# Attention and two expert layers on one core: the first expert weights' loads and the first two narrowed weight units are placed later in the attention

## The chip, the cores and the metric

One core of a Trainium2 chip. The metric is the device time in microseconds (us) of one execution of the whole program. The median of three runs of the kernel before is 1269.96 us (1268.87 to 1276.14).

The engines are named TensorE (PE in the rows, PEld for its weight loads), VectorE (DVE), ScalarE (ACT), GpSimd (POOL) and SP, the sync engine, which here only issues DMAs. Each engine works through its own list of instructions in order; semaphores make it wait for others.

## The reference

The program computes three layers in a row, in float32:

```python
scores = q @ k.T / 8                         # 4 batches x 8 heads, 576 x 576, head size 64
kth = 32nd largest of each row               # keep the 32 largest scores of a row
attn = softmax(where(scores >= kth, scores, -1e9)) @ v
x = attn as 2304 rows x 512
# layer 2: top-1 of 8 experts (512 -> 1024 relu -> 512), for rows with x @ w_skip > 0
e = argmax(x @ w_gate); y = softmax(..)[e] * (relu(x @ w1[e]) @ w2[e]); x = x + y
# layer 3: 512 -> 1536 -> 512, gated
out = (silu(x @ moe2_gate) * (x @ moe2_val)) @ moe2_out
```

The three weight matrices of layer 3 reach the kernel as 64-bit floats. The kernel must turn them into 32-bit ones itself.

## The kernel before

**Attention.** Heads are taken in pairs. There are 16 pairs (4 batches x 4) and 9 tiles of 128 score rows in each, so 144 tiles. Batches 0 and 1 are group 0 (tiles 0 to 71), batches 2 and 3 are group 1. For each tile, `head` (lines 213 to 220) computes the scores on TensorE into PSUM, and ScalarE copies them out (`sc`, L219). Then `rows_tile` (lines 222 to 262) finds the 32 largest of each row: VectorE takes the larger of the two halves (L230), GpSimd computes the smaller (L244, L245), and VectorE goes four times through top-8 (L235, L248), with a match-replace in between that strikes out what was found (L247). For tiles 0 to 80 the mask is then made on ScalarE and TensorE (L255, L259, L260). `late` transposes the weights and multiplies by v. At most three tiles' scores are made ahead.

`prep` (lines 113 to 169) is a generator that loads k and q of a pair (`load`, L123 the first 512 rows of a head, L131 the rest), splits them in two parts on GpSimd (L157, L160, L161), transposes them, and at the end loads v (L123, L129). It is started nine tiles ahead: at tile 36 for the pair that begins at tile 45. It then goes one step a tile, so that v is loaded five tiles after k and q.

**The order.** The program is written as one stream, tile by tile, and each piece gets its priority by its place in the stream. A scheduler then makes the list of each engine before the run. It takes what is ready by its own model of the times, the oldest first; so an instruction that waits for nothing can come much earlier in its list than its place in the program. `issue_after(i)` binds the instructions of a block on the engine of `i` to come behind `i` in that engine's list. It does not make them wait for its end, and it binds no other engine.

**The driver.** `run` (lines 615 to 705) pulls the attention forward. Its first loop (lines 641 to 651) covers tiles 0 to 80. Once per tile, after the tile's work, it adds other work:

- *Narrowed units.* Layer 3's weights are cut into 18 units. `split_gated` and `gated_unit` (lines 563 to 594) make one unit: two loads of 512 KB of 64-bit words (L581), three VectorE instructions that turn them into 32-bit floats (`narrow`, L611 to L613), a rounded copy on ScalarE (L590), the remainder on GpSimd (L591), and two stores into a DRAM scratch `w2s` (L593 the whole, L592 the two parts). The first ND1 = 2 units are made in the first loop, in one buffer named `dec`, so that the second's loads wait for the first's stores. Before, unit 0 is asked for ahead of tile 0 (line 637) and unit 1 at tile 1 (line 645). The other units are made in the second part.
- *First weights.* `whole_weights` (lines 596 to 605) loads 1 MB of the first expert into one of four buffers of the ring `whl` (L604). Four such loads are asked for at tiles 40 to 43 (lines 648 and 649). Nothing else uses these buffers before, and nothing in the program binds the loads to a place.

From tile 81 on a second loop mixes the rest of the attention with group 0's experts (`moe1_whole`), the other units and group 0's layer 3 (`moe2`). After the attention come group 1's experts (`moe1`, whose weights are loaded as `wraw`) and group 1's layer 3.

Of the kernel before, what the change touches and what calls it, by code (L numbers as in the profile page):

```python
# [16 lines left out]
P = 128  # L17
NEG = -3.0e38
# [14 lines left out]
class Kernel:  # L33
# [79 lines left out]
    def prep(self, R, b, h):  # L113

        nc, sb, D, S = self.nc, self.at, self.D, self.S

        first = self.npair == 0

        def load(nm, t, i, parts=(0, 1)):
            src, eng = self.a[nm], nc.sync  # L120
            o = src.offset + (b * self.H + h + i) * S * D
            if 0 in parts:
                eng.dma_start(t[:, i, :4, :].rearrange("p c d -> p (c d)"),  # L123
                              bass.AP(tensor=src.tensor, offset=o, ap=[[4 * D, P], [1, 4 * D]]))
            if 1 not in parts:
                return
            tail = bass.AP(tensor=src.tensor, offset=o + 512 * D, ap=[[D, 64], [1, D]])
            if nm == "v":
                eng.dma_start(t[:64, i, 4, :], tail)  # L129
            else:  # L130
                eng.dma_start(t[i * 64:(i + 1) * 64, 0, 4, :], tail)  # L131

        kT = [sb.tile([P, S], F32R, name="kT", bufs=4) for _ in range(2)]
        qT = [sb.tile([P, 2, 512], F32R, name="qT", bufs=4) for _ in range(2)]
        qt = self.qt[self.npair % 2]
        self.npair += 1
        R.update(kT=kT, qT=qT, qt=qt)
        raws = {nm: sb.tile([P, 2, 5, D], F32, name="raw", bufs=2) for nm in ("k", "q")}
        for nm in ("k", "q"):
            load(nm, raws[nm], 0)  # L140
            load(nm, raws[nm], 1, (1,))
        for nm in ("k", "q"):
            load(nm, raws[nm], 1, (0,))
        nat = None
        for i in range(2):
            for nm, w in (("k", 2), ("q", 3)):
                if nat:
                    self.prep_t(*nat)
                n = 5 - i
                t = sb.tile([P, 5, 3 * D], F32R, name="nat", bufs=1)  # L150
                o = t[:, :n, :w * D].rearrange("p c (t e) -> p c t e", t=w)
                src = raws[nm][:, i, :n, :]
                if first:
                    for z in range(0, w, 2):
                        nc.scalar.activation(o[:, :, z, :], src, AF.Copy)
                elif w == 3:
                    nc.gpsimd.tensor_scalar(o[:, :, 0:3:2, :], src[:, :, None, :].to_broadcast([P, n, 2, D]),  # L157
                                            1.0, 1.0, op0=OP.mult, op1=OP.mult)
                else:
                    nc.gpsimd.tensor_scalar(o[:, :, 0, :], src, 1.0, 1.0, op0=OP.mult, op1=OP.mult)  # L160
                (nc.vector if first else nc.gpsimd).tensor_tensor(o[:, :, 1, :], src, o[:, :, 0, :].bitcast(F32),  # L161
                                                                  op=OP.subtract)
                nat = (nm, i, t, kT, qT, qt)
                yield
        self.prep_t(*nat)
        yield
        R["v"] = raw = sb.tile([P, 2, 5, D], F32, name="vv", bufs=3)
        for i in range(2):
            load("v", raw, i)
# [52 lines left out]
    def rows_tile(self, R, i, c, Z, on_pe, sc):  # L222
        nc, S = self.nc, self.S
        sb = self.at1 if on_pe else self.at
        W = S // 2
        scf = sc.rearrange("p a b -> p (a b)")
        rest = sb.tile([P, 2, W], F32, name="rest", bufs=3)
        hj, lo = rest[:, 0], rest[:, 1]
        hi = sb.tile([P, W], F32, name="hi", bufs=3)
        nc.vector.tensor_tensor(hi, sc[:, 0, :], sc[:, 1, :], op=OP.max)  # L230
        pair, n = divmod(self.nlx, 9)
        tops = self.tops[pair % 2]
        h, kth = tops[:, n, :], tops[:, n, 31:32]
        self.nlx += 1
        nc.vector.max(h[:, 0:8], hi)  # L235
        nb = sb.tile([P, 1], F32, name="nb", bufs=5)
        nc.gpsimd.tensor_scalar(nb, h[:, 0:1], -0.125 / BIG, 1.0, op0=OP.mult, op1=OP.mult)
        pp = sb.tile([P, S], F32, name="pp", bufs=3)
        if not on_pe:
            e = sb.tile([P, S], F32, name="e", bufs=2)  # L240
            nc.scalar.activation(e, scf, AF.Exp, bias=nb, scale=0.125 / BIG)
        sm = sb.tile([P, W], I32, name="sm", bufs=2)
        sci = sc.bitcast(I32)
        nc.gpsimd.tensor_tensor(sm, sci[:, 0, :], sci[:, 1, :], op=OP.add)  # L244
        nc.gpsimd.tensor_tensor(lo.bitcast(I32), sm, hi.bitcast(I32), op=OP.subtract)  # L245
        for j in range(1, 4):
            nc.vector.match_replace(hj, h[:, (j - 1) * 8:j * 8], hi if j == 1 else hj, NEG)  # L247
            nc.vector.max(h[:, j * 8:(j + 1) * 8], hj if j < 3 else rest.rearrange("p a b -> p (a b)"))  # L248
        if n == 8:
            nc.gpsimd.tensor_tensor(self.FL[:, self.nlx - 9:self.nlx], tops[:, :, 23], tops[:, :, 31], op=OP.subtract)  # L250
        if not on_pe:
            nc.vector.scalar_tensor_tensor(pp, scf, kth, e, op0=OP.is_ge, op1=OP.mult, accum_out=Z)  # L252
            return pp
        u = sb.tile([P, 2, W], F32R, name="e", bufs=3)
        nc.scalar.activation(u, sc, AF.Relu, bias=kth, scale=-1.0)  # L255
        pS = self.ps1.tile([P, 2, 512], F32, name="pM", bufs=1)
        self.scores(R, i, c, pS, stop=False)
        for x in range(2):
            nc.tensor.matmul(pS[:, x, :W], self.nidr, u[:, x, :], start=False, stop=True)  # L259
        nc.scalar.activation(pp.rearrange("p (a b) -> p a b", a=2), pS[:, :, :W], AF.Exp, bias=nb, scale=0.125,  # L260
                             accum_out=Z)
        return pp
# [352 lines left out]
    def run(self):  # L615
        nc = self.nc
        with ExitStack() as st:
# [5 lines left out]
            ring = Ring(self.pool(st, "ring"), 0, 4)  # L623
            with ExitStack() as s1:
                tmp = self.pool(s1, "tmp")
                self.at1 = self.pool(s1, "attn1")
                self.nidr = self.at1.tile([P, P], F32R, name="nidr")
                nc.vector.tensor_scalar(self.nidr, self.idn, -1.0, None, op0=OP.mult)
                self.ps1 = self.psum_pool(s1, "ps1")
                self.rps = (self.ps1, "pR", 1)  # L630
                w = None

                def early():
                    nonlocal w
                    self.late_constants(tmp)
                    w = self.split_gated(tmp, range(ND1), ("dec",))
                    next(w)

                self.early = early
                ready = []  # L640
                for t, f in att:
                    if f < 1:
                        continue
                    if t % 2:
                        next(w, None)
                    if t == half + 8:
                        break
                    if t >= 40 and len(ready) < 4:
                        ready.append(self.whole_weights(ring, 0, len(ready)))
                for _ in w:  # L650
                    pass
            mo = Moe(self, self.pool(st, "moe"), self.psum_pool(st, "pm"), 3, ring, 2)
# [6 lines left out]
            w = self.split_gated(mo.mo, mid, ("h2h", "h2l"))  # L659
# [554 lines left out]
```

## Time and profile before

| | |
|---|---|
| median of three runs | 1269.96 us (1268.87 to 1276.14) |
| the profiled execution, whole | 1265.73 us |
| its span, first to last instruction | 1264.0 us |
| mean granted TensorE clock | 0.980 |
| TensorE busy | 1195.6 us (95%) |
| VectorE busy | 994.6 us (79%) |
| ScalarE busy | 741.2 us (59%) |
| GpSimd busy | 684.8 us (54%) |
| mean DMA rate | 173 GB/s |

The shares are over the whole span and hide that stages have different limits. Tiles 0 to 80 take about the first 325 us. An idle time is put down to what ended it last. TensorE's ends are modelled, so that a TensorE that reads 100% may still have room.

### The profile page before, as it was taken

To read this page: it belongs to the slowest core of one execution; us is meant where nothing else is said; L and a number is where in the kernel's file an instruction comes from. 1 tells how busy PE (TensorE), PEld (TensorE's weight loads), DVE (VectorE), ACT (ScalarE), POOL (GpSimd) and SP (SyncE) were. 2 spreads that over 40 slices of the span, in tenths; PEclk is the share of its full clock that TensorE was granted. 3 is DMA by queue.
4 is the path that set the end of the run, shared out by engine and by line. 5 is a ranking of instruction groups with operands and counts; after the bars stand their busy time and mean duration, and the time that the engine had idled before them with its cause. 6 is when DMAs were issued, how large, how long until landed. Compare 5 with 4: busy or idle time off the path is not lost. (4 is left out here: it accounts for less than half of the span.)

```text
span 1264.0 us, 21890 instructions
## 1 busy us (share of the span) xinstructions
PE 1195.6 (95%) x7365; PEld 1026.5 (81%) x7366; DVE 994.6 (79%) x2327; ACT 741.2 (59%) x1622; POOL 684.8 (54%) x825
## 2 busy tenths in 40 slices
PE   5999999999899989999999999989999999999995
PEld 4778887788687868787877788779998789898994
DVE  6999999999998888989999974247887458184570
ACT  5899988999754545555544453137776435343430
POOL 6776766777654666556766553121221535555550
PEclk9999999999999999999998999989999999999998
DMA  6511111111277879865667755598988544543420
GB/s 205 181 39 39 39 39 39 34 36 38 78 257 278 288 267 300 283 206 188 225 235 243 274 189 164 187 329 263 305 277 277 175 156 132 166 134 118 147 78 28
DMA packets 126012, 219.10 MB, mean 173 GB/s; under 512 B 17860, under 2 KB 84420, under 8 KB 119620
## 3 DMA queue, kind: packets, MB, share of 16 engines
q1 hardware_dynamic: 118868, 178.84, 43.5%
q0 software_dynamic: 7024, 38.78, 9.3%
q8 instruction: 60, 0.98, 0.3%
q14 instruction: 60, 0.49, 0.1%
HBM read 177.75 MB, written 41.95 MB: 174 GB/s over the span
## 5 line engine op out<-in xcount | busy, mean ns | idle before, releaser
L248 DVE MAX8 tops<-rest 128x8 f32<-128x288 f32 (+1 forms) x432 | 231.2, 546 | 5.7 <-POOL rest L245 2.3
L1139 PE MATMUL m<-x2h,whl 128*128 128x384 f32 x576 | 197.3, 343 | 3.8 <-DVE th L1148 2.0
L1140 PE MATMUL m<-x2l,whl 128*128 128x384 f32 x576 | 195.8, 340 | 0.4 <-DVE x2l L1125 0.4
L1141 PE MATMUL m<-x2h,whl 128*128 128x384 f32 x576 | 196.0, 341 | 0.0
L1108 POOL TENSOR_TENSOR whl<-wfly,whl 128x1024 fp32r<-128x1024 f32 x54 | 129.8, 2404 | 107.4 <-ACT whl L1107 107.2
L244 POOL TENSOR_TENSOR sm<-sc 128x288 int32<-128x288 int32 x144 | 124.5, 865 | 61.9 <-ACT sc L219 58.8
L245 POOL TENSOR_TENSOR rest<-sm,hi 128x288 int32<-128x288 int32 x144 | 125.0, 868 | 53.5 <-DVE hi L230 43.7
L271 ACT ACTIVATE pt<-pT 128x512 f32<-128x512 f32 (+2 forms) x320 | 115.9, 404 | 37.0 <-PE pT L269 35.3
L1107 ACT ACTIVATE whl<-wfly 128x1024 fp32r<-128x1024 f32 x69 | 73.2, 1061 | 98.5 <-PE m L1141 59.0
L247 DVE MATCH_REPLACE8 rest<-tops,rest 128x288 f32<-128x288 f32 x288 | 125.9, 438 | 0.0
L280 PE MATMUL pT<-pt,vv 128*64 128x256 f32 (+3 forms) x640 | 121.1, 424 | 4.9 <-DVE L L441 2.9
L269 PE MATMUL pT<-idn,pp 128*128 128x128 f32 (+1 forms) x720 | 119.3, 281 | 1.0 <-ACT kT L186 0.5
L219 ACT ACTIVATE sc<-pS 128x576 f32<-128x576 f32 x144 | 93.4, 649 | 44.4 <-DVE pp L252 27.9
L1139 PEld LDWEIGHTS m<-x2h,whl 128*128 128x128 f32 x576 | 109.3, 190 | 7.0 <-DVE th L1148 2.6
L269 PEld LDWEIGHTS pT<-idn,pp 128*128 128x128 f32 (+1 forms) x720 | 79.7, 137 | 39.0 <-issue 26.9
L1141 PEld LDWEIGHTS m<-x2h,whl 128*128 128x128 f32 x576 | 109.6, 190 | 1.5 <-issue 1.3
L1140 PEld LDWEIGHTS m<-x2l,whl 128*128 128x128 f32 x576 | 109.3, 190 | 1.5 <-DVE x2l L1125 0.6
L209 PE MATMUL pS<-kT,qT 128*128 128x288 f32 x512 | 106.4, 326 | 1.7 <-ACT sc L219 0.9
L944 DVE TENSOR_TENSOR whl<-wraw,whl 128x1024 fp32r<-128x1024 f32 x64 | 78.4, 1239 | 34.8 <-ACT whl L943 34.2
L230 DVE TENSOR_TENSOR hi<-sc 128x288 f32<-128x288 f32 x144 | 96.5, 670 | 11.1 <-ACT sc L219 10.8
L1151 DVE TENSOR_TENSOR h2l<-th,h2h 128x384 fp32r<-128x384 f32 x36 | 85.9, 2386 | 21.5 <-ACT h2h L1150 21.5
L943 ACT ACTIVATE whl<-wraw 128x1024 fp32r<-128x1024 f32 x64 | 67.1, 1059 | 38.6 <-DMA wraw<-in_moe_w_dram 23.8
(213 smaller groups left out, 2885.4 us busy)
## 6 DMA issues: line engine op xcount, KB each, us to landing
wfly<-w2s SPq DMA_DIRECT2D x69, 512.0 KB, 3.7
whl<-in_moe_w_dram SPq DMA_DIRECT2D x32, 1024.0 KB, 7.5
wraw<-in_moe_w_dram SPq DMA_DIRECT2D x64, 512.0 KB, 5.1
whl<-w2s POOLq DMA_DIRECT2D x31, 1024.0 KB, 5.7
w2s<-h2h SPq DMA_DIRECT2D x8, 1024.0 KB, 6.1
w2s<-whl SPq DMA_DIRECT2D x8, 1024.0 KB, 8.5
io<-xa SPq DMA_DIRECT2D x18, 256.0 KB, 3.0
out_dram<-io SPq DMA_DIRECT2D x18, 256.0 KB, 3.6
```

The source lines that it names most:

```text
L209: m = self.nc.tensor.matmul(pS[:, x, :W], l, r[:, x * W:(x + 1) * W], start=(n == 0), stop=stop and n == len(ops) - 1)
L244: nc.gpsimd.tensor_tensor(sm, sci[:, 0, :], sci[:, 1, :], op=OP.add)
L245: nc.gpsimd.tensor_tensor(lo.bitcast(I32), sm, hi.bitcast(I32), op=OP.subtract)
L247: nc.vector.match_replace(hj, h[:, (j - 1) * 8:j * 8], hi if j == 1 else hj, NEG)
L248: nc.vector.max(h[:, j * 8:(j + 1) * 8], hj if j < 3 else rest.rearrange("p a b -> p (a b)"))
L269: self.anchor = nc.tensor.transpose(p[:k, c - a, :], pp[:, c * P:c * P + k], self.idn)
L271: nc.scalar.activation(T[:k, a:z, do:do + n], p[:k, :z - a, so:so + n], AF.Copy)
L280: self.anchor = nc.tensor.matmul(po[(n % 2) * D:(n % 2 + 1) * D, :W], v[:k, i, n, :], T[:k, n, :W], start=(n < 2), stop=(n >= 3))
L1108: self.fly_engine.tensor_tensor(lo, raw, hi.bitcast(F32), op=OP.subtract)
L1139: nc.tensor.matmul(pz, wh[:, z, k, :], xh[:, k, :], start=(k == 0), stop=False)
L1140: nc.tensor.matmul(pz, wh[:, z, k, :], xl[:, k, :], start=False, stop=False)
L1141: nc.tensor.matmul(pz, wl[:, z, k, :], xh[:, k, :], start=False, stop=(k == 3))
```

## The change

Unit 0 and unit 1 are no longer asked for ahead of tile 0 and at tile 1, but after tiles 22 and 31. The four loads keep their tiles, 40 to 43. Both now stand in a block with two bindings: what the block gives to SP comes, in SP's list, behind the last long load of a head traced so far (`self.loaded`), and what it gives to VectorE comes, in VectorE's list, behind the last match-replace traced so far (`self.mark`).

At tile 22 `self.loaded` is the last q load of the pair that begins at tile 27, at tile 31 that of the pair of tile 36, at tile 40 that of the pair of tile 45; at tiles 41 to 43 it is the second head's v load of the pair of tile 45.

```diff
@@ prep / load
             if 0 in parts:
-                eng.dma_start(t[:, i, :4, :].rearrange("p c d -> p (c d)"),
-                              bass.AP(tensor=src.tensor, offset=o, ap=[[4 * D, P], [1, 4 * D]]))
+                self.loaded = eng.dma_start(t[:, i, :4, :].rearrange("p c d -> p (c d)"),
+                                            bass.AP(tensor=src.tensor, offset=o, ap=[[4 * D, P], [1, 4 * D]]))
@@ rows_tile
         for j in range(1, 4):
-            nc.vector.match_replace(hj, h[:, (j - 1) * 8:j * 8], hi if j == 1 else hj, NEG)
+            self.mark = nc.vector.match_replace(hj, h[:, (j - 1) * 8:j * 8], hi if j == 1 else hj, NEG)
@@ run
                     w = self.split_gated(tmp, range(ND1), ("dec",))
-                    next(w)
...
                 for t, f in att:
                     if f < 1:
                         continue
-                    if t % 2:
-                        next(w, None)
+                    with self.tc.issue_after(self.loaded.ins), self.tc.issue_after(self.mark.ins):
+                        if t in (22, 31):
+                            next(w, None)
+                        if t >= 40 and len(ready) < 4:
+                            ready.append(self.whole_weights(ring, 0, len(ready)))
                     if t == half + 8:
                         break
-                    if t >= 40 and len(ready) < 4:
-                        ready.append(self.whole_weights(ring, 0, len(ready)))
```

## Rows read from the trace of the kernel before

**Rows 1.** The page's 40 slices of 31.6 us, tenths busy: VectorE.

```profile
DVE  6999999999998888989999974247887458184570
```

**Rows 2.** Waits of VectorE, 13 to 330 us: us in total, times, longest.

```profile
DVE hi L230 <- ACT sc L219: 5.2, 2, 5.1
```

**Rows 3.** Stretches: us, busy us (instructions) of the five, TensorE clock, DMA share, GB/s.

```profile
46.00:54.00 8.00, 8.00 (x58) 6.04 (x58) 8.00 (x16) 7.56 (x20) 6.66 (x8) 1.00 0.15 36
54.00:72.00 18.00, 15.99 (x113) 12.49 (x110) 18.00 (x59) 15.79 (x44) 15.38 (x25) 1.00 0.31 114
72.00:106.00 34.00, 34.00 (x255) 27.50 (x255) 34.00 (x108) 31.40 (x87) 24.63 (x42) 1.00 0.14 37
210.00:290.00 80.00, 79.35 (x595) 64.76 (x594) 80.00 (x254) 74.77 (x200) 58.23 (x98) 1.00 0.14 38
```

**Rows 4.** Stretch 210 to 290 us, L235 alone: us, VectorE busy (instructions), clock, DMA.

```profile
210.00:290.00 80.00, 9.79 (x22) 1.00 0.14 38
```

**Rows 5.** Tile dec, to 130 us: ns min/median/max, first and last start.

```profile
L611 DVE TENSOR_SCALAR dec<-dec x2: 681/940/1198, 18.8 to 46.1; 128x1024 int32<-128x1024 int32 x2
L612 DVE SCALAR_TENSOR_TENSOR dec<-dec x2: 1214/1271/1328, 21.1 to 48.4; 128x1024 int32<-128x1024 int32 x2
L613 DVE SCALAR_TENSOR_TENSOR dec<-dec x2: 1883/1888/1893, 24.4 to 51.5; 128x1024 int32<-128x1024 int32 x2
...
L590 ACT ACTIVATE dec<-dec x2: 1051/1054/1058, 26.3 to 53.4; 128x1024 fp32r<-128x1024 f32 x2
L591 POOL TENSOR_TENSOR dec<-dec x2: 2347/2364/2380, 28.2 to 55.4; 128x1024 fp32r<-128x1024 f32 x2
```

**Rows 6.** Lines L611, L612 and L613, whole span: the later units.

```profile
L611 DVE TENSOR_SCALAR h2h<-h2h x8: 669/694/1290, 339.6 to 517.5; 128x1024 int32<-128x1024 int32 x8
...
L612 DVE SCALAR_TENSOR_TENSOR h2h<-h2h x8: 1202/1216/1264, 342.1 to 519.3; 128x1024 int32<-128x1024 int32 x8
...
L612 DVE SCALAR_TENSOR_TENSOR whl<-whl,one x8: 1203/1267/1829, 578.7 to 702.6; 128x1024 int32<-128x1024 int32 x8
...
L613 DVE SCALAR_TENSOR_TENSOR h2h<-h2h x8: 1205/1210/1966, 345.0 to 521.5; 128x1024 int32<-128x1024 int32 x8
```

**Rows 7.** GpSimd by line, 72 to 140 us: busy us, mean ns, idle before.

```profile
L245 POOL TENSOR_TENSOR rest<-sm,hi 128x288 int32<-128x288 int32 x19 | 15.2, 803 | 7.5 <-DVE hi L230 7.5
```

**Rows 8.** SP's issues in order of time, 20 to 42 us: start us, us.

```profile
20.79 4.63 SPq L604 DMA_DIRECT2D whl<-in_moe_w_dram  x4
...
30.54 0.34 SPq L592 DMA_DIRECT2D w2s<-dec  x1
39.64 0.38 SPq L581 DMA_DIRECT2D dec<-in_moe_w_gate_dram  x1
```

**Rows 9.** Tile whl: landing of the first four loads (to 130 us); first reader.

```profile
DMA to landing us min/median/max: 10.7/11.8/13.0
...
L1072 PE MATMUL m<-whl,x2l x64: 379/379/634, 348.6 to 381.6; 128*128 128x256 f32 x64
```

**Rows 10.** Order of time: SP's issues 139 to 181 us, GpSimd's first use.

```profile
147.22 0.58 SPq L123 DMA_DIRECT2D raw<-in_q_dram  x1
...
167.24 0.58 SPq L123 DMA_DIRECT2D vv<-in_v_dram  x1
...
171.90 0.33 SPq L123 DMA_DIRECT2D raw<-in_k_dram  x1
...
184.75 0.46 POOL L160 TENSOR_SCALAR nat<-raw 128x320 fp32r<-128x320 f32 x1 [0.96 <-PE pR L185]
```

**Rows 11.** Stretch 30 to 40 us, columns as in rows 3.

```profile
30.00:40.00 10.00, 9.42 (x55) 7.96 (x56) 10.00 (x33) 8.69 (x19) 6.85 (x11) 0.75 0.84 303
```

**Rows 12.** TensorE in order of time, 24 to 33 us: [idle before <-releaser].

```profile
30.55 0.85 PE L259 MATMUL pM<-e,nidr 128*128 128x288 f32 x2 [3.78 <-ACT e L255]
```

**Rows 13.** Waits of SP's queue, to 180 us: us in total, times, longest.

```profile
SPq L410 <- DVE rz L408: 15.9, 1, 15.9
```

**Rows 14.** The chain that ended last: start us, us, what.

```profile
828.14 15.12 DMA wraw<-in_moe_w_dram
```

## The prediction

> **What bounds the kernel now.** The change touches only the first 81 of the 144 attention tiles, so the first question is which engine sets their pace. I read the page's slices first: VectorE is at nine tenths or more in every slice from the second to the thirteenth, which ends near 410 us [rows 1]. Then the waits of VectorE alone from 13 to 330 us: there is one entry, 5.2 us, and 5.1 of it is the first score tile's arrival [rows 2]. After that VectorE never waits for anybody for 300 us. The table by stretches says the same: 18.00 of 18.00, 34.00 of 34.00 and 80.00 of 80.00 us busy, while GpSimd and ScalarE have slack [rows 3]. TensorE shows 100% in two of these stretches too, but its ends are modelled, and it is short of that (15.99 of 18.00) where VectorE is not. So this stage is a queue of VectorE work. Its pace is the count of the first top-8 of each tile: 22 in 80 us, 3.64 us a tile [rows 4].
>
> **What the change moves, part 1: two narrowed units.** A unit costs VectorE three instructions (L611, L612, L613), ScalarE 1.05 us, GpSimd 2.36 us, and SP four DMAs: two loads, two stores. Before, both units lie between 18.8 and 58 us. Removed from there on VectorE: (0.681 + 1.198) + (1.214 + 1.328) + (1.883 + 1.893) = 8.2 us [rows 5]. All of it lies on the path, as the queue has no gap there: tiles 0 to 12 will be done up to 8.2 us earlier.
>
> The same six instructions come back behind the last match-replace of tiles 22 and 31, near 100 and 133 us. The queue is full there as well, so they are paid again. Their price is bounded by the later units of the same shape: at least 0.669 + 1.202 + 1.205 = 3.08 us a unit, at most 1.290 + 1.829 + 1.966 = 5.09 us [rows 6], for two units 6.2 to 10.2 us. The net of removal and return is therefore between -2.0 and +2.0 us. The long forms go with a busy GpSimd, and that is 85% busy (15.38 of 18.00) at 54 to 72 us, where the start still catches up, but 72% (24.63 of 34.00) where the units go [rows 3]. So I take -1 us.
>
> On L613 the two units took 1.89 us against 1.21 us at best, 0.68 us more, and a GpSimd instruction of a tile takes 0.80 us [rows 5 to 7]. The Trainium skill (SBUF — State Buffer, section "SBUF: two separate sides") has a rule for that: a VectorE instruction with two SBUF inputs and a GpSimd instruction that reads SBUF lock the same ports for a whole instruction, and the later one waits. The row agrees, being longer by less than one GpSimd instruction. By the rule alone, with none of L612 and L613 delayed before and all four delayed by a whole GpSimd instruction after, the sum would be 4 x 0.80 = 3.2 us the other way, an estimate with that page's lock.
>
> The rest of a unit is covered. ScalarE's 1.05 us and GpSimd's 2.36 us fall into stretches where these have 2.6 and 9.4 us free of 34 [rows 3]; uncovered, they would cost at most 2 x (1.05 + 2.36) = 6.8 us. The unit at 46 to 58 us is the nearest case of one placed into the running stage: VectorE had no gap there (8.00 of 8.00, then 18.00 of 18.00). TensorE was idle for 2 us afterwards and nobody lost by it [rows 3].
>
> SP issues its queue in order. Before, the second store of a unit was issued at 30.54 us, SP then stood until 39.64 us for the stores to land, as the one buffer has to be free, and only then came the next unit's loads [rows 8]. After the change the same standing falls behind tile 22. What is queued behind it is the next heads' q loads, then the tiny reciprocal load and the x stores. Loads of raw k at 171.90 us are read by GpSimd at 184.75 us [rows 10], so these loads run 10 us or more ahead, as much as SP stood. I cost it at nothing.
>
> **Part 2: the four 1 MB loads.** They were issued from 20.79 us, took 10.7 to 13.0 us to land, and nobody reads them before 348.6 us [rows 8, 9]. After the change the first can be issued right behind the q load at 147.22 us, the other three behind the v load at 167.24 us [rows 10]. Either place leaves some 170 us. Nothing at 20 to 33 us waits for a DMA that they delay, since VectorE has no gap, so their going gives nothing either. At the new place the raw k loads come behind three of them: three quarters of 13.0 us is 9.8 us, against the 12.8 us from issue to use. Hidden, with 3 us left; if that cover is gone, GpSimd stands and VectorE follows.
>
> **Part 3: clock and order.** Between 30 and 40 us the granted clock was 0.75 of full speed, half of that stretch at its lower level, 1.2 GHz instead of 2.4 [rows 11]. It fell after TensorE had waited 3.8 us, until 30.55 us, for a mask that VectorE made late, the narrowing being in between [rows 12]. The dip will be smaller or gone. That gives nothing, because VectorE did not wait for TensorE even then [rows 2]. From a profile of before no one can read how the list of instructions after tile 81 is re-sorted when the early part shifts; that is a rival below.
>
> **The sum.** The profiled execution took 1265.73 us (span 1264.0 and 1.7 around it). -8.2 + 7.2 (the units) + 0 (loads) + 0 (clock, SP) = -1.0, so 1264.7 us on its own scale. The median of the three runs shown is 4.2 us above that execution; on the scale of the median 1269 us. I forecast no change.
>
> **The rivals.** Times are on the median's scale; about 1% (12.7 us, so 1257.3 and 1282.7) is what a measurement of this kernel tells from no change.
>
> A, the start keeps its gain. If at tiles 22 and 31 TensorE and not VectorE set the pace, the 8.2 us would be hidden there: 1270 - 8.2 = 1262. For it: TensorE reads 34.00 of 34.00 at 72 to 106 us. Against it: a VectorE that is not the bound would wait, and it does not [rows 2]. 14%.
>
> B, VectorE stands in front of the second unit. The buffer is single, so unit 1 loads only after unit 0's stores have landed. In the trace of before from L613 of unit 0 (24.4 us, end 26.3) to L611 of unit 1 (46.1 us) went 19.8 us [rows 5]. From L611 to L611 lie nine tiles and one unit after the change, 9 x 3.64 + 4.1 = 36.9 us; less 7.3 us from L611 to the end of L613 (46.1 to 53.4 us for unit 1), 29.6 us are left, a margin of 9.8 us. SP's longest single wait is 15.9 us, for the reciprocals of a finished pair [rows 13], and one such wait falls between the two units. If SP puts the loads behind it, they are late by up to 15.9 - 9.8 = 6 us, and if the stores of unit 0 fall behind one too, by 6 + 9.8 = 16 us. VectorE's queue is in order, so it loses just that: 1276 to 1286. It decides from the point where L611 waits for a DMA at all. 12%, a third of it beyond 1%.
>
> C, the second half is sorted anew. The order of instructions on each engine is made before the run, by priorities and modelled times; a shift of some us at the start can put other instructions first where attention and experts are mixed. The size is that of the largest single wait on the chain that a changed order could remove or repeat: 15.12 us, TensorE for the first raw weights of the second group's experts [rows 14]. Either way: 1254 or 1285. Against it: after tile 31 both programs have the same work behind them, so the later order should be nearly the same. 18%: 9% down beyond 1%, 4% up beyond 1%, the rest small.
>
> D, the change doesn't do what it says: the edge behind the match-replace holds VectorE's instructions only, so scalar copies, splits and stores follow by their data, but the six narrowing instructions cannot run early. This would end in no change too. It is inside the forecast.
>
> **The numbers.** The forecast, 56%, holds 1268 to 1272 by the bounds of the units, and 1266 to 1274 with a little of their ScalarE and GpSimd work uncovered. With A (14%), B and C: faster by over 1% 0.10 (9% from C, 1% from A with some of C), slower 0.08 (4% from B, 4% from C), within 1% 0.82. The range reaches from A's 1262 down to half of C's way, 1259, and up to B's lower end with some of the rest, 1280; it leaves out about a tenth on each side.
>
> **What would show it.** Right: tile 12 done some 8 us earlier, tile 35 done within 2 us of before, L611 to L613 near 100 to 140 us at 3.1 to 5.1 us a unit, VectorE with no wait of over 1 us between 20 and 330 us, the four loads landing after 148 us. TensorE's full clock at 30 to 40 us without effect would confirm part 3. Wrong: tile 35 done 5 us or more earlier (A), a wait of VectorE for a DMA before L611 (B), GpSimd waiting for raw k near 185 us (part 2's cover gone), or equal times up to 330 us and a difference that arises later (C).

## The result and the profile after

The changed kernel takes 1256.48 us (median of 12 runs, 1250.97 to 1261.86), the kernel before, run beside it, 1268.21 us (12 runs, 1261.10 to 1276.14). The ratio is 0.991, with a 95% interval of 0.989 to 0.9931. I had forecast 1269.0 in a range from 1259 to 1280, so the time lies 2.5 us below the range. The profiled execution has a span of 1252.2 us (before 1264.0), a mean granted clock of 0.983 (0.980) and TensorE busy for 1193.1 us (1195.6).

The first stage came out as predicted. VectorE's slices of the page after, 31.3 us each:

```profile
DVE  6999999999999998989999973248888358183670
```

VectorE's waits after, from 13 to 330 us (us in total, times, longest) give the same single entry as before [rows 2]:

```profile
DVE hi L230 <- ACT sc L219: 5.2, 2, 5.1
```

The stretches after, columns as in [rows 3], where they have their counterparts (also [rows 11]):

```profile
30.00:40.00 10.00, 9.95 (x73) 8.42 (x71) 9.82 (x31) 8.90 (x23) 7.11 (x12) 0.93 0.05 16
46.00:54.00 8.00, 7.94 (x59) 6.20 (x57) 8.00 (x26) 7.63 (x22) 6.82 (x12) 1.00 0.01 2
...
72.00:106.00 34.00, 33.87 (x256) 27.71 (x256) 33.94 (x101) 31.80 (x89) 26.76 (x39) 1.00 0.27 82
106.00:143.00 37.00, 36.57 (x270) 29.58 (x268) 37.00 (x112) 33.90 (x88) 30.06 (x45) 1.00 0.30 95
210.00:290.00 80.00, 79.83 (x597) 65.48 (x596) 80.00 (x251) 74.23 (x200) 56.82 (x97) 1.00 0.13 35
```

VectorE is still without a gap, and the same 22 first top-8s of L235 fall into 210 to 290 us as in [rows 4]:

```profile
210.00:290.00 80.00, 9.74 (x22) 1.00 0.13 35
```

The two units now (tile dec after; ns min/median/max, first and last start us), against [rows 5]:

```profile
L611 DVE TENSOR_SCALAR dec<-dec x2: 679/880/1080, 98.3 to 133.6; 128x1024 int32<-128x1024 int32 x2
L612 DVE SCALAR_TENSOR_TENSOR dec<-dec x2: 1202/1202/1203, 100.4 to 136.0; 128x1024 int32<-128x1024 int32 x2
L613 DVE SCALAR_TENSOR_TENSOR dec<-dec x2: 1216/1440/1664, 102.7 to 138.3; 128x1024 int32<-128x1024 int32 x2
```

Their sum is (0.679 + 1.080) + (1.202 + 1.203) + (1.216 + 1.664) = 7.0 us, against 8.2 before. I call a tile done when its last top-8, the one of 576 elements (L248, 0.75 us), ends. Tile 12 is done at 64.2 us (before 71.2), tile 35 at 152.5 (152.9), tile 80 at 325.6 (326.6). So the 7 us of the start are paid back, and 1.0 us is left. This is one execution of each, and 1.0 us is within what kernels with nearly the same first stage differ by: tile 80 is done at 324.4 us in units_only and at 329.2 us in loads_only (experiment 1). VectorE, around tile 80, before and then after (start us, us):

```profile
325.87 0.75 DVE L248 MAX8 tops<-rest 128x8 f32<-128x576 f32 x1
```

```profile
324.86 0.74 DVE L248 MAX8 tops<-rest 128x8 f32<-128x576 f32 x1
```

SP after, in order of time: the stores of unit 1 (L593, L592) and the four 1 MB loads (L604) behind a q load.

```profile
142.11 0.58 SPq L123 DMA_DIRECT2D raw<-in_q_dram  x1
142.79 0.38 SPq L593 DMA_DIRECT2D w2s<-dec  x1
143.22 2.12 SPq L604 DMA_DIRECT2D whl<-in_moe_w_dram  x3
145.44 4.63 SPq L592 DMA_DIRECT2D w2s<-dec  x1
150.11 0.44 SPq L604 DMA_DIRECT2D whl<-in_moe_w_dram  x1
```

**Where the 12 us arise.** Behind tile 80 attention and the first group's experts share the engines, and TensorE is the busiest. One row of stretches from 330 to 520 us shows it (columns as in [rows 3]), before and then after:

```profile
330.00:520.00 190.00, 176.60 (x1028) 143.10 (x1026) 169.90 (x414) 97.19 (x227) 114.78 (x139) 0.96 0.80 268
```

```profile
330.00:520.00 190.00, 183.32 (x1088) 148.82 (x1088) 179.65 (x436) 105.86 (x247) 128.88 (x152) 0.98 0.85 283
```

In the same 190 us TensorE gets through 60 matrix instructions more. It idles 6.7 us instead of 13.4, and by the clock's records it runs 6.8 us at 1.2 GHz instead of 13.7, which is 3.4 us of work more. Together that is 10.1 us; with the 1.0 us of tile 80 it makes 11.1 of the 11.8 us by which the spans differ.

The traces also tell where the lead is complete. TensorE's last 4087 of its 7365 records are the same instructions in the same order before and after; they begin at 518.9 us before and at 505.8 us after, so the changed kernel is 13.1 us ahead there. The row of six L287 just behind that point, before and then after:

```profile
519.36 0.81 PE L287 MATMUL pT<-fold,oT 128*128 128x64 f32 x6
```

```profile
506.19 0.81 PE L287 MATMUL pT<-fold,oT 128*128 128x64 f32 x6
```

From there to the end the changed kernel takes 746.4 us and the kernel before 745.0, so about 1.3 us of the lead is lost again behind it. TensorE's waits from 345 to 510 us (us in total, times, longest), before:

```profile
PE m L1054 <- ACT th L1076: 4.7, 2, 3.4
PE m L1054 <- DMA io<-xa,ids: 4.5, 4, 2.5
```

and after:

```profile
PE m L1054 <- DMA io<-xa,ids: 1.8, 2, 1.3
PE pS L209 <- ACT sc L219: 1.8, 2, 1.5
PE m L1085 <- ACT x2h L1057: 1.0, 1, 1.0
```

The two largest waits of before, in order of time: the transposes of an expert's gathered rows (`io`), and those of its first layer's result (`th`), stand in TensorE's list before their input is there, and hold up what follows them.

```profile
389.93 1.03 PE L1054 MATMUL m<-idn,io 128*128 128x128 f32 x4 [2.53 <-DMA io<-xa,ids]
...
468.85 1.12 PE L1054 MATMUL m<-idn,th 128*128 128x128 f32 x4 [3.40 <-ACT th L1076]
```

### The profile page after: what moved, and what is told of

The parts are those of the page before. It is cut to its first block, busy times and chain, and to the rows that moved or that the text cites. A ratio compares the mean times of both kernels' runs of the same rounds, so it can differ in the third digit from the quotient of the medians.

```text
span 1252.2 us, 21888 instructions
## 1 busy us (share of the span) xinstructions
PE 1193.1 (95%) x7365; PEld 1024.1 (82%) x7366; DVE 990.3 (79%) x2327; ACT 742.4 (59%) x1622; POOL 690.6 (55%) x825
## 5 line engine op out<-in xcount | busy, mean ns | idle before, releaser
L248 DVE MAX8 tops<-rest 128x8 f32<-128x288 f32 (+1 forms) x432 | 230.8, 546 | 3.4
L1148 DVE SCALAR_TENSOR_TENSOR th<-th,m 128x384 f32<-128x384 f32 x72 | 39.1, 543 | 64.1 <-ACT th L1147 64.1
```

## The experiments

Ratios are to the kernel before, run beside each group (1267.6 to 1269.5 us), with 95% intervals. Diffs are against the changed kernel unless said otherwise. Kernels of different groups are best compared by these ratios, as the kernel before itself differs by up to 1.9 us between the groups. "Unit places" are the tiles behind which the two narrowed units are asked for (22 and 31 in the changed kernel).

**1. The units alone, and the loads alone.**

```diff
 units_only: the four loads as in before
-                        if t >= 40 and len(ready) < 4:
-                            ready.append(self.whole_weights(ring, 0, len(ready)))
...
+                    if t >= 40 and len(ready) < 4:
+                        ready.append(self.whole_weights(ring, 0, len(ready)))
 loads_only: the units as in before
+                    next(w)
...
+                    if t % 2:
+                        next(w, None)
-                        if t in (22, 31):
-                            next(w, None)
```

> Units at tiles 22 and 31 as in the changed kernel; the four 1 MB loads unbound as before. The lists of VectorE, TensorE, ScalarE and GpSimd are then those of the changed kernel, instruction for instruction; only SP's differs. Theory (the units' place re-sorts the lists, so that group 0's routing ends earlier and the experts start near 339 us instead of 349): within 3 us of the changed kernel, 1256, ratio to before 0.991. Rival (the gain is the 4 MB that no longer load at 20 to 33 us): 1266 to 1270, ratio 1.000.

> The two units at the start as before; only the four 1 MB loads bound behind the heads' loads. The routing stands at the same place in VectorE's list as before (the gates' product L541 after 85 tiles' first maxima). Theory: 1264 to 1271, ratio 1.000, first expert matmul within 3 us of 348.6 us. Rival (the loads' place is the gain): 1254 to 1260.

Measured: units_only 1255.87 us, 0.9894 [0.9867, 0.9921]; loads_only 1267.21 us, 0.9996 [0.9977, 1.0016]. The whole gain comes with the units' move, and the place of the four loads is worth nothing, as part 2 of the prediction had it. In units_only the lists of TensorE, VectorE, ScalarE and GpSimd are those of the changed kernel, instruction for instruction; only SP's differs.

**2. Later experts.** After the change the routing of group 0 and so the first expert's matrix instruction come earlier, at 338.9 us against 348.6 [rows 9]. Tile whl after, to 360 us:

```profile
L1072 PE MATMUL m<-whl,x2l x32: 378/379/483, 338.9 to 347.5; 128*128 128x256 f32 x32
```

My first theory was that this start carries the gain.

```diff
-            yield from self.first_slots(g, b, oh, sl, rows, gw)
+            yield from (*[0] * (3 * (g == 0 and b == 1)), *()); yield from self.first_slots(g, b, oh, sl, rows, gw)
...
-        nc.vector.tensor_tensor(v[:, :, :, 1], oh, gate...)                       # L541
+        with self.tc.issue_after(self.masked.ins) if (g, b) == (0, 1) else ExitStack(): (L541 as it was)
```

(`self.masked` is the last L252 traced.)

> The changed kernel with one instruction bound: the gates' product L541 of group 0's second batch comes in VectorE's list behind the masked weights L252 of the next tile, as it did in the kernel before. The lists are the same as in the changed kernel up to that instruction. Theory (the chain from this instruction over the first slots, the row numbers and the gather starts the experts): first expert matmul 5 to 8 us later than 338.9 us, the whole 4 to 8 us above the changed kernel, 1260 to 1264. Rival (the experts' start has slack, the gain is elsewhere): no change, 1256.

Measured: 1257.54 us, 0.9914 [0.9889, 0.9939]. The first expert instruction starts at 350.5 us, 11.6 us later than in the changed kernel, and the ratio is the same (0.991):

```profile
350.52 1.75 PE L1072 MATMUL m<-whl,x2l 128*128 128x256 f32 x7
```

This theory fell: an early start of the experts is not what carries the gain.

**3. Other places for the units.**

```diff
-                        if t in (22, 31):
+                        if t in (31, 40):   # units_31_40;  (40, 49), (49, 58), (61, 70), (13, 22) likewise
```

> The changed kernel with the units at tiles 31 and 40 instead of 22 and 31. By the lists the routing falls one tile later than in the changed kernel (L541 after 85 tiles' first maxima, as before). Theory (the routing's place in the list decides, whatever brings it there): first expert matmul near 346 to 350 us, 1263 to 1270. Rival (units anywhere behind the start give the gain, because the pause of VectorE lets TensorE catch up): 1254 to 1258.

> The changed kernel with the units at tiles 49 and 58. By the lists the row numbers of group 0 (L557) stand where they stand in the changed kernel, after 85 tiles' first maxima and 83 finished tiles, one tile ahead of before. Theory (the place of the routing in the list decides): TensorE's work at 400 us at least 6 us ahead of before, 1254 to 1261. Rival (TensorE's catching up behind tiles 22 and 31 is what counts, as 31 and 40 were slow): 1266 to 1274.

> The changed kernel with the units at tiles 61 and 70. By the lists L557 stands after 85 first maxima and 82 finished tiles, the earliest of all. Theory: first expert matmul at 342 us or earlier, TensorE's work at 400 us at least 8 us ahead of before, 1250 to 1260. Rival (a pause of VectorE so near to the end of the stage is not made up for, and the experts start later): 1264 to 1272.

> The changed kernel with the units at tiles 40 and 49. By the lists L557 stands after 86 first maxima and 84 finished tiles, as before and as with the units at 31 and 40. Theory: no gain, TensorE's work at 400 us within 6 us of before, 1263 to 1273. Rival (any place behind the start but the one tried gives the gain): 1253 to 1260.

> The changed kernel, with the two units behind tiles 13 and 22 instead of 22 and 31. In VectorE's list the routing step L541 stands behind the same tile as in the changed kernel. If that place goes with the gain (it does in the changed kernel, with the units alone moved, and with tiles 49 and 58): 1253 to 1260. If it is only the accident of where the lists interleave: between 1254 and 1273, most likely nearer 1268, as four of the seven placements so far are. Up to 320 us tile 80 is done within 2 us of the changed kernel either way.

Measured: 31 and 40: 1272.70 us, 1.0028 [1.0007, 1.0049]. 49 and 58: 1258.41, 0.9916 [0.9886, 0.9946]. 61 and 70: 1268.99, 1.0001 [0.9974, 1.0029]. 40 and 49: 1268.94, 0.9999 [0.9974, 1.0025]. 13 and 22: 1258.28, 0.9892 [0.9849, 0.9936]. The gain comes and goes with no trend in the place. In all five the units are gone from the start, and in three of them there is no gain: that the start carries it falls with these. With 61 and 70 the first expert instruction is at 342.6 us, earlier than in before, and nothing is gained, against a forecast of 1250 to 1260. With 31 and 40 the time came out above the forecast of the theory and of its rival. So neither the place of the units nor the routing's decides by itself.

**4. A shorter first stage.** Of the three narrowing instructions only the first is left for the two moved units. (A first form of this edit, short_narrow, gave no result.)

```diff
+            self.narrow(words..., one.bitcast(I32), u < ND1)
...
     nc.vector.tensor_scalar(t, high, 3, ...)      # L611
+    if short: return
```

> The changed kernel, with only the first of the three narrowing instructions (L611) for the two moved units: their weights are wrong, the work behind them is all there. It takes two times (1.20 + 1.44) = 5.3 us of VectorE's work out of the first stage. If that stage is a queue of VectorE's work, as predicted, tile 35 is done 5.3 us earlier than in the changed kernel, and tiles 70 and 80 still 4 to 6 us earlier. For the total: if the stage's time goes through to the end, 1249 to 1253; if the order of the lists behind it decides (they differ from tile 25 on), anything from 1246 to 1272, and no relation to the 5.3 us.

Measured: 1259.75 us, 0.9911 [0.9882, 0.9941]. Tile 35 is done 3.9 us earlier than in the changed kernel, tile 70 5.1 us, tile 80 3.7 us:

```profile
321.10 0.75 DVE L248 MAX8 tops<-rest 128x8 f32<-128x576 f32 x1
```

Taking 5.3 us of VectorE's work out shortens the first stage by 3.7 to 5.1 us, at tiles 35 and 80 less than forecast, but far from nothing: it is a queue of VectorE's work. The end gains nothing by it (0.9911 against the changed kernel's 0.991). TensorE reaches the common records, the last 4087, at 511.3 us, 5.5 us behind the changed kernel, so the 3.7 us that it was ahead at tile 80 were lost between there and this point.

**5. Only the order changed, with the start kept.** The routing step of group 0's second batch gets a raised priority, in the kernel before and in the changed one.

```diff
 reorder_from_before (against before), reorder_from_after (against the changed kernel)
-                side.append(self.finish_pair(g, b, j, X[w], Z[w]))
+                side.append(self.finish_pair(g, b, j, X[w], Z[w])); hot.extend(side[-1:] * ((g, b, j) == (0, 1, NP - 1)))
...
-            with self.tc.high_priority(200) if t in preps else ExitStack():
+            with self.tc.high_priority(200) if t in preps + hot else ExitStack():
```

> The kernel before, with the routing step of the first group's second batch raised in priority. Units and loads stay where they were; VectorE's list is that of before up to the first top-8 of tile 83, and differs from there on. Theory (the order of the lists behind the first stage sets the 12 us, whatever the start does): up to about 330 us the trace is that of before within 1 us; behind it TensorE's idle gaps and its time at 1.2 GHz change, and the total moves with them, by 3 us or more in either direction (1255 to 1265 or 1272 to 1280), with the change in (idle + half of the time at 1.2 GHz) equal to the change of the span within 5 us. Rival (only the start, tiles 1 to 31, carries the gain): 1266 to 1271, as before.

> The changed kernel, with the same raise in priority of the routing step. VectorE's list is that of the changed kernel up to tile 82, and differs from there on. Theory (order behind the first stage): equal to the changed kernel within 1 us up to about 320 us, and then the total moves by 3 us or more in either direction (1244 to 1253 or 1260 to 1275), by what TensorE's idle gaps and its time at 1.2 GHz change. Rival (the start carries the gain): 1253 to 1259, as the changed kernel.

Measured: reorder_from_before 1272.57 us, 1.0018 [0.9993, 1.0043], which is not told from no change. reorder_from_after 1267.42 us, 0.9990 [0.9961, 1.0019]. It has the changed kernel's list of VectorE up to tile 82, its tile 80 is done at 325.9 us (325.6), and the gain is gone. Its profiled execution was one of its quicker ones (span 1259.2); even so TensorE is busy for 175.28 us between 330 and 520 us and not 183.32:

```profile
330.00:520.00 190.00, 175.28 (x1035) 142.10 (x1035) 178.24 (x421) 101.37 (x234) 120.34 (x144) 0.98 0.80 273
```

with a new wait in order of time, for GpSimd's split of a head:

```profile
430.00 0.53 PE L185 MATMUL pT<-idr,nat 128*128 128x128 f32 x4 [2.86 <-POOL nat L161]
```

The rival that the start carries the gain fell with this too. With the same raise the two kernels still differ by 5.2 us, and their late orders differ as well; what part of that the start has is not shown.

**6. The late list as the predictor.** The lists of instructions of these kernels, compared instruction by instruction, showed that some share all of TensorE's and VectorE's late list, that is, all of it from some tile of the attention on. So I built three whose late list was already known from another kernel, and forecast each by that alone.

```diff
-                        if t in (22, 31):
+                        if t in (4, 13):    # units_4_13;  (0, 1) in units_0_1
 routing_held
-            yield from self.first_slots(g, b, oh, sl, rows, gw)
+            yield from self.first_slots(g, b, oh, sl, rows, gw) if (g, b) != (0, 1) else self.held(0, g, b, oh, sl, rows, gw)
+def held(self, n, *args):          # its first instructions come behind the last match-replace traced
+    with self.tc.issue_after(self.mark.ins):
+        it = self.first_slots(*args); next(it)
+    yield; yield from it
```

> The changed kernel, with the two units behind tiles 4 and 13. The lists of instructions come out like this: VectorE's from tile 50 on, and TensorE's from there on, are instruction for instruction those of the kernel with the units at 13 and 22, and from tile 90 those of the changed kernel. Theory (the order of the lists from the first group's routing to the last attention tile sets the time, wherever the units lie): 1254 to 1260, with the changed kernel's waits of TensorE behind 345 us: none over 2 us up to 500 us. Rival (what the start keeps or gives back sets it): by the changed kernel's gain of 8 us at tile 12 given back later, no order of lists matters, and with a unit as early as before's it would be nearer 1264 to 1270.

> The changed kernel, with the two units behind tiles 0 and 1, so that their place is nearly that of before. VectorE's and TensorE's lists from tile 44 on are those of the kernel before, instruction for instruction. Theory (order of the lists): 1264 to 1272, with before's waits of TensorE at 378, 390 and 469 us, shifted by a few us at most. Rival (the edges that hold the loads and units behind other instructions, or the loads' place, bring the 12 us by themselves): 1254 to 1260.

> The changed kernel, with the routing step of the first group's second batch held behind the last match-replace of tile 47. Units and loads are those of the changed kernel, and so are the lists up to tile 47; from tile 85 on the lists are those of the kernel whose routing was raised in priority from before. Theory (order of the lists): up to 320 us as the changed kernel within 2 us; then that other kernel's time of 1268 to 1277 with its holes of TensorE (342, 379, 409, 474 us). Rival (the start carries the gain): 1253 to 1260.

Measured: units_4_13 1259.68 us, 0.9941 [0.9925, 0.9958]; units_0_1 1269.92 us, 1.0002 [0.9984, 1.0020]; routing_held 1267.88 us, 0.9987 [0.9961, 1.0012], 0.1 us below its forecast's lower end. Each total came out with its list. Not all of the rest did: routing_held has tile 70 done 3.1 us later than the changed kernel, not within 2 us, and only two of its four forecast holes (378.8 and 409.8 us); of before's three waits units_0_1 has those at 390 and 469 us (391.9 and 470.8, 2.2 and 1.6 us long), that at 378 us is down to 0.5 us, and one of 1.9 us at 502.8 us is new. The same stretch of units_4_13, units_0_1 and routing_held:

```profile
330.00:520.00 190.00, 178.93 (x1071) 145.52 (x1070) 179.90 (x437) 103.43 (x240) 125.33 (x148) 0.99 0.83 278
```

```profile
330.00:520.00 190.00, 174.35 (x1019) 141.31 (x1018) 169.41 (x419) 97.88 (x229) 114.14 (x140) 0.96 0.79 265
```

```profile
330.00:520.00 190.00, 175.03 (x1024) 140.94 (x1023) 170.85 (x432) 100.60 (x232) 114.77 (x140) 0.96 0.77 262
```

The families, by the tile from which VectorE's list is the same (TensorE's is from about there or earlier):

```
late list shared                                    times, us
changed kernel, units_only (whole), 13_22           1256.5, 1255.9, 1258.3,
  (from tile 90), 4_13 (as 13_22 from tile 50)        1259.7
before, units_0_1 (from tile 44), loads_only        1268.2, 1269.9, 1267.2
units_31_40, units_40_49 (from tile 77)             1272.7, 1268.9
reorder_from_before, routing_held (from tile 85)    1272.6, 1267.9
```

The first family stands apart; the other three, with three different orders, are not told from one another by these times. Kernels with the same list have most of their longer waits at nearly the same place, though their units lie up to 18 tiles apart. The changed kernel, units_13_22 and units_4_13, each in order of time:

```profile
453.94 0.80 PE L209 MATMUL pS<-kT,qT 128*128 128x288 f32 x4 [1.52 <-ACT sc L219]
```

```profile
457.31 0.80 PE L209 MATMUL pS<-kT,qT 128*128 128x288 f32 x4 [1.53 <-ACT sc L219]
```

```profile
459.41 0.80 PE L209 MATMUL pS<-kT,qT 128*128 128x288 f32 x4 [1.53 <-ACT sc L219]
```

and units_31_40 and units_40_49, two waits that the changed kernel has not:

```profile
344.08 1.30 PE L269 MATMUL pT<-idn,pp 128*128 128x128 f32 x5 [5.48 <-DVE pp L252]
...
416.45 0.75 PE L185 MATMUL pT<-idr,nat 128*128 128x128 f32 x4 [3.78 <-POOL nat L161]
```

```profile
343.03 1.30 PE L269 MATMUL pT<-idn,pp 128*128 128x128 f32 x5 [4.37 <-DVE pp L252]
...
415.19 0.75 PE L185 MATMUL pT<-idr,nat 128*128 128x128 f32 x4 [4.03 <-POOL nat L161]
```

Where the deciding stretch ends can be read from the traces of all 18 profiled kernels. In twelve of them, before and the changed kernel among them, TensorE's last 4087 records stand in the same order. They begin between 505.6 and 522.5 us (units_49_58 508.1, before 518.9, units_61_70 520.9), and from there every one of the twelve takes 745.0 to 751.4 us. In all 18 the last 2589 records are the same; they begin between 764.6 and 783.7 us, and the rest takes 487.4 to 492.0 us. So most of the differences between these kernels arise ahead of the common part, before about 520 us in the twelve. What differs behind it is of the size that two kernels with the same lists show: units_only reaches the point at 505.6 us, 0.2 us from the changed kernel, and then takes 751.4 us where that takes 746.4. The first of the 2589, before and then after, where the lead (11.8 us) is that of the whole span:

```profile
776.60 0.44 PE L1140 MATMUL m<-x2l,whl 128*128 128x384 f32 x1
```

```profile
764.84 0.44 PE L1140 MATMUL m<-x2l,whl 128*128 128x384 f32 x1
```

**7. The order alone, from before.** In VectorE's list of the kernel before, the first top-8 of tile 83 (or 84) is bound behind the routing step L541.

```diff
 against before; order_84 with (84,)
-        nc.vector.max(h[:, 0:8], hi)
+        with self.tc.issue_after(self.gates.ins) if self.nlx - 1 in (83,) else ExitStack(): nc.vector.max(h[:, 0:8], hi)
...
+        self.gates = nc.vector.tensor_tensor(v[:, :, :, 1], oh, gate...)          # L541
```

> The kernel before with one binding: in VectorE's list the first top-8 of tile 83 comes behind the routing step L541 of the first group. Units and loads stay at before's place, and VectorE's list is that of before up to tile 84. Behind some 200 instructions that stand in another order the list is again almost that of before, and TensorE's last 4874 instructions are in the order of both kernels. Theory (order of the lists between the routing and about 520 us): up to 334 us as before within 1 us; then the total may leave 1269 with no unit or load moved, towards 1258 where TensorE's holes at 378, 390 and 469 us go, and by as much as these change. Rival (the gain needs the units' move): 1266 to 1272.

> The same binding one tile later: the first top-8 of tile 84 behind the routing step L541. Its list differs from that of order_83 only between tile 84 and the end of the attention. Theory (order of the lists): up to 334 us as before within 1 us, and a time of its own, between 1254 and 1275, which goes with TensorE's idle time and its time at 1.2 GHz behind 334 us within 5 us. Rival (the gain needs the units' move): 1266 to 1272.

Measured: order_83 1267.35 us, 0.9977 [0.9954, 1.0000]; order_84 1270.48 us, 1.0013 [0.9985, 1.0042]. Neither is told from no change (the interval of order_83 just reaches 1). That another order takes the gain away is shown (5 and 6); that an order brings it to the kernel before, with no unit moved, is not.

**TensorE's account.** Over the 18 profiled kernels, from 330 us to TensorE's last record, I added TensorE's idle time (the gaps between its records) and half of its time at 1.2 GHz. Before has 36.2 + 30.7/2 = 51.6 us, the changed kernel 30.0 + 27.3/2 = 43.6, units_31_40 40.2 + 47.8/2 = 64.1. Against the spans the sum has a correlation of 0.89 and a slope of 0.93 us for a us. TensorE has the same instructions to get through in all of them, so this is in good part book-keeping: it says where the time lies, in holes of TensorE and in its slower clock, and not why one order has fewer.

## Why the prediction was wrong

**The first stage: right.** "a queue of VectorE work" held: VectorE has no new wait, its pace is the same, and experiment 4 shows the stage following VectorE's work. The sum of the units was -1.0 us (-8.2 + 7.2); it was 7.0 instead of 7.2 returned, and tile 80 came 1.0 us earlier. That tile 80 agrees this well is in part luck, as it differs by more between kernels with nearly the same first stage. Tile 12 was 7.0 us early where I wrote some 8. GpSimd was 79% busy where the first unit went (26.76 of 34.00 us), busier than the 72% I had taken from before, and still only one L611 (1.08 us against 0.68) and one L613 (1.66 against 1.22) came out long. The Trainium skill's rule (SBUF — State Buffer, section "SBUF: two separate sides") would have made the stage up to 3.2 us longer by my estimate; the trace doesn't show that, since three of the four L612 and L613, which could lose the ports by that estimate, took 1.20 to 1.22 us and so lost nothing.

**The loads: right in effect, off in place.** Three of them went out at 143.2 us, the fourth at 150.1 us behind unit 1's second store, and not behind the v load at 167.24 us. I had misread that row: it is the v load of the pair of tile 54. The one that binds the loads, that of the pair of tile 45, was issued at 134.41 us before and at 130.14 us after. That cost nothing (experiment 1).

**The clock at 30 to 40 us: right.** It rose from 0.75 to 0.93 and gave nothing at tile 35. One reading was off: the clock did not fall behind the wait that ends at 30.55 us but within it, as it is at 0.50 from 28.4 us on.

**The failed step is in part 3**: "From a profile of before no one can read how the list of instructions after tile 81 is re-sorted when the early part shifts", which I put at nothing in the sum, and the argument against rival C: "after tile 31 both programs have the same work behind them, so the later order should be nearly the same." The work is the same, the order is not: in the traces VectorE's records of before and after part after the first 27 of 2327 and stand in one order again only in the last 820, from 545.8 and 532.5 us on; TensorE's part after 81 and meet again in the last 4087. In between the changed kernel gains its lead of 13.1 us, 1.0 us of it by tile 80 and the rest while TensorE goes through 330 to 520 us. That order, which I had put at nothing, was worth 10 to 12 us. It is what I had named as the sign of C: "equal times up to 330 us and a difference that arises later". I gave C 18%, and 9% to its side below 1257.3 us.

**C's size came near by luck, for a wrong reason.** I had priced it by the 15.12 us wait for the second group's first raw weights [rows 14]. That wait is still there, 14.20 us in the chain after:

```profile
817.84 14.20 DMA wraw<-in_moe_w_dram
```

The 11.8 us are made of many waits of 0.5 to 3.4 us and of the clock. A price that the profile of before did show is the idle time and the time at 1.2 GHz between 330 and 520 us, 13.4 + 6.8 = 20 us, by my estimate the most that a better order of that stretch could bring. The other placements came out on both sides, from 11 us below to 5 us above the median of the kernel before beside them.

**What stays open.** Which property of an order makes it good. The place of L541 in VectorE's list goes with the gain in the eight placements of the two units that ran (with it, behind the last top-8 of tile 80: 22/31, 13/22, 4/13, 49/58; without it, a tile earlier: 61/70, a tile later: 31/40, 40/49, 0/1). But gates_later has it a tile later and keeps the gain, and reorder_from_after has it behind tile 80 and loses it. The runs don't tell what in the whole stretch decides, and no run brought the gain to the kernel before without moving a unit.

## What to carry to other kernels

When a program is sorted by a scheduler before the run, an edit of its early part can also be a new draw of the order in its later part. Price that draw from the idle time and the slow-clock time of the stretch where different streams of work are mixed, put it into the range on both sides, and expect that it can be larger than the edit itself: here the draws lay from 12 us below to 5 us above the kernel before, and the edit's own sum was 1 us. Before a gain is put down to an edit's purpose, make a variant that keeps the edit and changes only the late order: if the gain goes, it belonged to the order, and the next edit may lose it again.

## What was not expected of the hardware

TensorE's granted clock goes with the holes. In before it is full through the 3.4 us wait that ends at 468.85 us, and at half, 1.2 GHz, in the 3.4 us behind, in which TensorE works again (columns as in [rows 3]):

```profile
465.40:468.50 3.10, 0.06 (x1) 0.00 (x0) 3.00 (x10) 0.96 (x2) 1.46 (x3) 1.00 1.03 370
...
468.60:472.00 3.40, 3.15 (x10) 2.70 (x11) 3.33 (x9) 2.70 (x9) 3.37 (x4) 0.50 0.58 196
```

In the kernel before, whose longest waits behind 345 us are 2.5 and 3.4 us, TensorE ran 13.7 us at 1.2 GHz between 330 and 520 us. In units_31_40, with waits of 5.5 and 3.8 us, it was 27.3 us (granted mean 0.93), and in units_4_13, whose longest wait there is 1.8 us, 3.4 us (0.99). So a wait of TensorE can cost more than its own length: in units_31_40 the slower clock adds up to 13.7 us (half of 27.3, an estimate) to 16.5 us of idle time in this stretch. The length of a wait alone does not tell it: gates_later has one of 3.7 us at 342 us, 13.7 us of idle time in all, and only 3.4 us at 1.2 GHz.
